# Early v products, DMA transposes for the second block, resident q and v weights, and parked q outputs in idle weight rows

## The chip, the cores and the metric

One core of one Trainium2 chip. The metric is the device time of one execution in microseconds (us); the time of a kernel is the median of its runs. A profiled span is about 2 us shorter than the time of the same run (730.3 of 732.26 for the kernel before).

The granted clock is TensorE's clock in the records, as a share of full speed: 1.0 is full.

Engines: PE is TensorE, DVE VectorE, ACT ScalarE, POOL GpSimd, SP SyncE (here it only issues DMAs).

## The reference

```python
xn = layernorm(x)                      # x: 1 x 2048 x 1024, bf16
q, k, v = split(xn @ wqkv)             # 32 heads of 32
logits = q . k[pos - 2*w], w = 0..7    # sliding window, 8 keys at distance 2
s = (softmax(logits * 32**-0.5) @ v[pos - 2*w]) @ wo
g = silu((silu(xn @ w1) * (xn @ w3)) @ w2)   # hidden width 3584
return x + s * g
```

## The kernel before

The rows of x are worked on in four blocks of 512 (numbered 0 to 3). Every large product is done with Strassen-Winograd: seven half-size products in place of eight, at the price of operand sums on DVE. PE computes q, k and v for blocks 0 and 1, then for blocks 2 and 3, then the MLP for the first 1024 rows, then the second. The attention is not on PE: its scores and weighted values are elementwise work on DVE, laid between other DVE instructions.

Outputs of blocks 1 to 3 are *parked* in DRAM, through a pool of staging buffers (`k4`) that everything else uses too:

```python
def park(t, c, j0, name):                       # t: 0 q, 1 k, 2 v;  c: block
    tl = k4(name, (2, CH), BF16)
    dst = (q_dram, k_dram, v_dram)[t][c, :, j0:j0 + 2, :]
    def fin():
        nc.sync.dma_start(out=dst, in_=tl[:])
    return tl[:], fin
```

How attention work gets its place in DVE's order is settled when the program is built. A generator yields the estimated time of each attention instruction; each PE group grants a budget, and other DVE work is charged to it as `owed`:

```python
def qkv_sums(w0, w1_, st):
    ...                                         # four sums on DVE
    pace["owed"] += 4.5
def bg(us):
    ...
    pace["credit"] += us - pace["owed"]
    pace["owed"] = 0
    with priority(BG), behind("v"):
        while pace["credit"] > 0:
            t = next(att_it)                    # places one DVE instruction
            ...
            pace["credit"] -= t
```

Of the kernel before, what the change touches and what calls it, by code (L numbers as in the profile page):

```python
# [8 lines left out]
FP32 = mybir.dt.float32  # L9
BF16 = mybir.dt.bfloat16  # L10
# [7 lines left out]
def kernel(  # L18
# [11 lines left out]
    nc = tc.nc  # L30
    P = 128
    S, D, F = 2048, 1024, 3584
    Dh, W, DIL = 32, 8, 2
    KT = D // P
    KH = KT // 2
    CH = 512
    NC = S // CH
    NST = CH // P
# [4 lines left out]
    NJ = 8  # L43
    NR = 4
    BG = 1000000
    I = range(2)
# [36 lines left out]
        out=ident[:], in_=ident[:], compare_op=ALU.not_equal, fill=1.0,  # L83
# [5 lines left out]
        out=ones4[:], in_=ones4[:], compare_op=ALU.is_ge, fill=0.0,  # L89
# [3 lines left out]
        out=ones4[:], in_=ones4[:], compare_op=ALU.is_ge, fill=0.0,  # L93
# [5 lines left out]
        out=maskb[0:32], in_=maskb[0:32], compare_op=ALU.is_ge, fill=-1.0e9,  # L99
# [9 lines left out]
    oT = keep.tile([P, 2, NJ, CH], BF16, name="oT")  # L109
    o16 = oT[:].bitcast(FP16)  # L110
    pb = keep.tile([P, W, P], BF16, name="pb")
    xT = keep.tile([P, 3, KH, CH], BF16, name="xT")
    xs = keep.tile([P, 4, KH, CH], FP16, name="xs")
# [4 lines left out]
    def slot(i, shape, dt=BF16, at=0):  # L118
        n = 1
        for x in shape:  # L120
            n *= x
        v = wring[:, i:i + max(1, n // SLOT), :].rearrange("p s n -> p (s n)")[:, at:at + n]
        v = v if dt is BF16 else v.bitcast(dt)
        d = "abc"[:len(shape)]
        return v.rearrange(f"p ({' '.join(d)}) -> p {' '.join(d)}", **dict(zip(d, shape)))

    def rows(f0, n, dt=BF16):
        v = h_sb[:, f0:f0 + n, :].rearrange("p f n -> p (f n)")
        return v if dt is BF16 else v.bitcast(dt)
# [4 lines left out]
    def k4(name, shape=(2, CH), dt=FP32):  # L134
        return kk.tile([P, *shape], dt, tag="k4", name=name)
# [93 lines left out]
    xt = {}  # L229
# [11 lines left out]
    def ln_dve(c, sts):  # L241
        xt4 = xt[c]
        n = len(sts)
        mv = small.tile([P, n, nc.vector.BN_AGGR_DIM], FP32, tag="mv")
        rstd = small.tile([P, n], FP32, tag="rstd")
        for i, st in enumerate(sts):
            stats = small.tile([P, 2, nc.vector.BN_STATS_DIM], FP32, tag="stats")
            for h in range(2):
                nc.vector.bn_stats(out=stats[:, h, :], in_=xt4[:, st, h * 512:(h + 1) * 512])
            nc.vector.bn_aggr(out=mv[:, i, :], in_=stats[:])  # L250
        nc.scalar.activation(out=rstd[:], in_=mv[:, :, 1], func=ACTF.Sqrt, bias=eps_t[:], scale=1.0)
        nc.vector.reciprocal(out=rstd[:], in_=rstd[:])
        for i, st in enumerate(sts):
            nc.vector.tensor_scalar(
                out=xt4[:, st, :], in0=xt4[:, st, :], scalar1=mv[:, i, 0:1], scalar2=rstd[:, i:i + 1],
                op0=ALU.subtract, op1=ALU.mult,
            )
# [18 lines left out]
    def ln_tp(c, st, dst, busy=0):  # L276
        tp = bank2(f"tp{c}_{st}")
        spin(tp, busy)
        for kt in range(KT):
            nc.tensor.matmul(  # L280
                tp[:, kt // KH, (kt % KH) * P:(kt % KH + 1) * P], lhsT=xt[c][:, st, kt * P:(kt + 1) * P], rhs=ident[:],
                start=(kt % KH == 0), stop=(kt % KH == KH - 1), skip_group_check=True,
            )
        cols = slice(st * P, (st + 1) * P)
        for d, s_ in dst:
            nc.scalar.copy(out=d[..., cols], in_=tp[:, s_].rearrange("p a (k t) -> p a k t", k=KH))
        return tp
# [5 lines left out]
    def xn_sums(b11, b21, b12, b22, o):  # L293
        nc.vector.tensor_sub(o[:, 0], b12, b11)
        nc.vector.tensor_sub(o[:, 1], b22, o[:, 0])
        nc.vector.tensor_sub(o[:, 2], b22, b12)
        nc.vector.tensor_sub(o[:, 3], b21, o[:, 1])
# [9 lines left out]



    def qkv_sums(w0, w1_, st):  # L310
        lo = lambda w: w.rearrange("p k (c two j) -> p k c two j", two=2, j=4)[:, :, :, 0]
        hi = lambda w: w.rearrange("p k (c two j) -> p k c two j", two=2, j=4)[:, :, :, 1]
        a11, a21, a12, a22 = lo(w0), hi(w0), lo(w1_), hi(w1_)
        s1, s2, s4 = [s.rearrange("p k (c j) -> p k c j", j=4) for s in st]
        s3 = hi(w0.bitcast(FP16))
        nc.vector.tensor_add(s1, a21, a22)
        nc.vector.tensor_sub(s2, s1, a11)
        nc.vector.tensor_sub(s4, a12, s2)
        nc.vector.tensor_sub(s3, a11, a21)
        pace["owed"] += 4.5  # L320

    def qkv_A(w0, w1_, st, g):
# [5 lines left out]
        sp = lambda q: [[sv[q][:, k, 2 * g + i, :] for k in range(KH)] for i in I]  # L328
        return pick(v0, 0), pick(v1, 0), pick(v1, 1), sp(0), sp(1), pick(v3, 1), sp(2)

    def park(t, c, j0, name):
        tl = k4(name, (2, CH), BF16)
        dst = (q_dram, k_dram, v_dram)[t][c, :, j0:j0 + 2, :]

        def fin():
            nc.sync.dma_start(out=dst, in_=tl[:])

        return tl[:], fin

    def qkv_dst(t, c, j0):  # L340
        if c == 0:
# [15 lines left out]
    def qkv_seven(t, b, w0, w1_, st, mid=None, snaps=None):  # L357
        c0, c1 = 2 * b, 2 * b + 1
        for g in range(2):
            cp = lambda c, j0: qkv_copy(t, c, j0)  # L360
            seven(f"q{t}{b}{g}", qkv_A(w0, w1_, st, g), Bq[b],
                  cp(c0, 2 * g), cp(c1, 2 * g), cp(c1, 4 + 2 * g), cp(c0, 4 + 2 * g),
                  None if snaps is None else snaps[g])
            if mid is not None:
                mid(g)

    def qkv_load(t, h, wt):
        anchor["wq"] = nc.sync.dma_start(out=wt, in_=wqkv_r[:, h * 4:(h + 1) * 4, t * D:(t + 1) * D])
        return wt
# [5 lines left out]
    def att_tile(shape, dt, name):  # L375
        return att.tile([P, *shape], dt, tag="a8", name=name)
# [6 lines left out]
    sc = {}  # L383
# [19 lines left out]
    def scores(c, ws):  # L403
        q = qt[c]
        if c not in sc:
            sc[c] = att_tile((W, CH), BF16, f"Es{c}"), att_tile((NJ, CH), BF16, f"pt{c}")
        E, p_t = sc[c]
        for w in ws:
            o = HALO - DIL * w
            nc.vector.tensor_mul(p_t[:], q[:], kT[:, :, o:o + CH])  # L410
            yield 2.3
            nc.vector.tensor_add(p_t[:, 0:4, :], p_t[:, 0:4, :], p_t[:, 4:8, :])  # L412
            yield 1.25
            nc.vector.tensor_add(p_t[:, 0:2, :], p_t[:, 0:2, :], p_t[:, 2:4, :])
            yield 0.7
            nc.vector.tensor_add(E[:, w, :], p_t[:, 0, :], p_t[:, 1, :])
            yield 0.45
# [102 lines left out]
    pace = {"n": 0, "credit": 0, "owed": 0}  # L520
# [36 lines left out]

    tiles = {}

    free = [0, 1, 2, 3, 4, 6, 7, 8, 9]  # L560
    half = [0, 1]
    held = {}

# [403 lines left out]
    wq0 = qkv_load(0, 0, slot(2, (4, D)))  # L967
    x_load(1)
    wq1 = qkv_load(0, 1, slot(6, (4, D)))
    for st in range(NST):  # L970
        (ln_act if st == 2 else ln_dve)(0, [st])
    qt[0] = att_tile((NJ, CH), BF16, "qt0")
    tps = [ln_tp(0, st, [], busy=(5, 0, 1, 1)[st]) for st in range(NST)]
    for a in I:
        for st in range(NST):
            (nc.vector.tensor_copy if st < 2 else nc.scalar.copy)(
                out=xT[:, a, :, st * P:(st + 1) * P], in_=tps[st][:, a].rearrange("p (k t) -> p k t", k=KH),
            )
    wk0 = qkv_load(1, 0, slot(8, (4, D)))
    wk1 = qkv_load(1, 1, rows(0, 4).rearrange("p (k n) -> p k n", k=4))  # L980
    sk = rows(4, 6, FP16).rearrange("p (q k n) -> p q k n", q=3, k=4)
    sk = [sk[:, q] for q in range(3)]
    b12 = k4("b12", (KH, CH), BF16)
    x_load(2)
    ln_dve(1, [0, 1])
    ln_dve(1, [2, 3])

    sq = rows(20, 6, FP16).rearrange("p (q k n) -> p q k n", q=3, k=4)
    sq = [sq[:, q] for q in range(3)]
# [1 line left out]
    Bq = B0, B_of(xT1[0], xT1[1], xT1[3], xs1)  # L991
    def tp1(*sts):
        for st in sts:
            ln_tp(1, st, [(b12[:].unsqueeze(1), slice(0, 1)), (xT[:, 2:3], slice(1, 2))])

    for t, (w0, w1_, ws) in enumerate(((wq0, wq1, sq), (wk0, wk1, sk))):
        first_two(f"f{t}", [qkv_A(w0, w1_, ws, g) for g in range(2)], B0[0], B0[1],
                  snap[2 * t:2 * t + 2], [qkv_copy(t, 0, 2 * g) for g in range(2)],
                  *((lambda: None, 4) if t == 0 else (lambda: tp1(2, 3), 0)))
        if t == 0:  # L1000
            tp1(0, 1)
    qkv_sums(wq0, wq1, sq)
    xn_sums(xT[:, 0], xT[:, 1], b12[:], xT[:, 2], xs)
    qkv_sums(wk0, wk1, sk)
    qkv_seven(0, 0, wq0, wq1, sq, None, snap[0:2])
    x_load(3)
# [4 lines left out]

    tr(2)

    wv = [slot(2 + 4 * h, (4, D)) for h in I]
    sva = slot(0, (2, 4, CH), FP16)
    sv = [sva[:, 0], sva[:, 1], rows(10, 2, FP16).rearrange("p (k n) -> p k n", k=4)]

    def before_v(g):
        if g == 0:
            for h in I:  # L1020
                qkv_load(2, h, wv[h])
            tr(3)
        else:
            with behind("v"):
                qkv_sums(*wv, sv)

# [5 lines left out]
                xn_sums(xT1[0], xT1[1], xT1[2], xT1[3], xs1)  # L1032
        w2_step()
    pace["n"] = PACE[0]
    qkv_seven(2, 0, *wv, sv, step0)
    pace["n"] = PACE[1]
    qkv_seven(1, 1, wk0, wk1, sk, step)
    flush()
    wq0 = qkv_load(0, 0, slot(8, (4, D)))
    wq1 = qkv_load(0, 1, rows(0, 4).rearrange("p (k n) -> p k n", k=4))  # L1040
    qkv_sums(wq0, wq1, sk)
    qkv_seven(2, 1, *wv, sv, step)
    qkv_seven(0, 1, wq0, wq1, sk, step)
    flush()
# [46 lines left out]
```

## Time and profile before

| | kernel before |
|---|---|
| time, median of 3 runs | 732.37 us (732.24 to 732.5) |
| span of the profiled run, granted clock | 730.3 us, 0.998 |
| PE busy | 714.2 us, 98% |
| DVE busy | 624.2 us, 85% |
| first qkv product / first product that needs the x sums | 13.25 / 29.57 us |
| first MLP product / first down-projection product | 161.46 / 417.75 us |
| last PE work ends | 724.30 us |

The times of the lower rows are starts of PE rows in order of time. The prediction shows the page, the waits and the rows that it rests on.

In a row in order of time the columns are start (us), duration (us), engine, line of the program, operation, output<-inputs, shapes and count; a bracket at the end gives the idle time just before and what ended it (`issue`: nothing that the row itself names). L149 is the helper that issues every product, L159 the helper for ACT copies, so tiles tell what a row is: `am`, `bm`, `em` are accumulators of the MLP's up products, `aq`, `bq`, `eq` (and `af`) of qkv, `da`, `db`, `de` of the down projection.

### The profile page before, as it was taken

To read this page: it belongs to the slowest core of one execution; us is meant where nothing else is said; L and a number is where in the kernel's file an instruction comes from. 1 tells how busy PE (TensorE), PEld (TensorE's weight loads), DVE (VectorE), ACT (ScalarE), POOL (GpSimd) and SP (SyncE) were. 2 spreads that over 40 slices of the span, in tenths; PEclk is the share of its full clock that TensorE was granted. 3 is DMA by queue.
4 is the path that set the end of the run, shared out by engine and by line. 5 is a ranking of instruction groups with operands and counts; after the bars stand their busy time and mean duration, and the time that the engine had idled before them with its cause. 6 is when DMAs were issued, how large, how long until landed. Compare 5 with 4: busy or idle time off the path is not lost.

```text
span 730.3 us, 8739 instructions
## 1 busy us (share of the span) xinstructions
PE 714.2 (98%) x3312; PEld 345.8 (47%) x3367; DVE 624.2 (85%) x677; ACT 314.5 (43%) x328; POOL 99.3 (14%) x159
## 2 busy tenths in 40 slices
PE   7999999999999999999999999999999999999996
PEld 4655665654444444444444444444444444444442
DVE  7994688878798879878989899969859999979984
ACT  5744343437554546654545411123454555120233
POOL 0000000010400110142202010010345000510011
PEclk9999999999999999999999999999999999999999
DMA  9379148877756452467755745549799453666505
GB/s 321 140 177 286 57 147 281 254 210 262 200 204 231 143 175 87 141 194 242 231 174 191 240 156 186 178 162 375 188 283 326 136 159 102 192 190 203 179 5 111
DMA packets 117610, 140.82 MB, mean 193 GB/s; under 512 B 14273, under 2 KB 91073, under 8 KB 116929
## 3 DMA queue, kind: packets, MB, share of 16 engines
q1 hardware_dynamic: 103984, 101.47, 44.9%
q0 software_dynamic: 13584, 38.81, 17.2%
q8 instruction: 26, 0.43, 0.3%
q14 instruction: 16, 0.12, 0.1%
HBM read 98.30 MB, written 38.80 MB: 188 GB/s over the span
## 4 chain that ended last, share of the span: by engine, by line
PE 71%; DVE 18%; DMA 4%; issue 3%; ACT 3%; SPq 1%; POOL 0%; DVEq 0%; ACTq 0%; POOLq 0%
PE bm L149 17%; PE am L149 11%; PE em L149 11%; PE db L149 7%; PE bq L149 5%; PE de L149 4%; DVE pt L410 4%; PE eq L149 4%; PE da L149 3%; PE aq L149 3%; PE wb L149 2%; DVE pt L412 2%; PE we L149 2%; PE wa L149 2%; DMA q_dram<-pk 1%
## 5 line engine op out<-in xcount | busy, mean ns | idle before, releaser
L149 PEld LDWEIGHTS <-wring 128*128 128x128 f16 (+1 forms) x1920 | 201.7, 105 | 216.4 <-issue 5.2
L149 PEld LDWEIGHTS <-h_sb 128*128 128x128 f16 (+1 forms) x1088 | 114.0, 105 | 121.7 <-issue 1.0
L149 PE MATMUL bm<-xs,wring 128*128 128x512 f16 x504 | 117.3, 379 | 0.5 <-DVE h_sb L661 0.3
L149 PE MATMUL am<-xT,wring 128*128 128x512 bf16 x322 | 78.8, 379 | 0.9
L410 DVE TENSOR_TENSOR pt<-qt,kT 128x4096 bf16<-128x4096 bf16 x32 | 73.2, 2288 | 0.7
L149 PE MATMUL db<-wring,h_sb 128*128 128x512 f16 x336 | 73.2, 379 | 0.0
L465 DVE TENSOR_TENSOR BC<-Ep,vT 128x2048 bf16<-128x2048 bf16 x56 | 67.0, 1218 | 0.2
L646 DVE TENSOR_TENSOR um<-em,um 128x1024 f32<-128x1024 f32 x28 | 34.2, 1222 | 19.9 <-PE em L149 12.9
L648 ACT ACTIVATE g<-um 128x1024 bf16<-128x1024 f32 x28 | 29.6, 1057 | 49.7 <-DVE um L646 49.7
L149 PE MATMUL da<-wring,h_sb 128*128 128x512 bf16 x219 | 48.9, 379 | 0.3
L451 POOL DMA_DIRECT2D Ep<-pb x64 | 37.9, 600 | 25.5 <-DVE pb L447 18.5
L149 PE MATMUL bm<-h_sb,wring 128*128 128x512 f16 x168 | 39.7, 379 | 0.0
L149 PE MATMUL em<-xs,wring 128*128 128x512 f16 x168 | 39.7, 379 | 0.0
L412 DVE TENSOR_TENSOR pt<-pt 128x2048 bf16<-128x2048 bf16 x32 | 39.1, 1221 | 0.5
L475 DVE TENSOR_TENSOR oT<-oT,BC 128x2048 bf16<-128x2048 bf16 x32 | 39.1, 1220 | 0.5
L149 PE MATMUL em<-xT,wring 128*128 128x512 bf16 x161 | 39.2, 379 | 0.3
L159 ACT COPY bm<-am 128x1024 f32<-128x1024 f32 x28 | 28.0, 999 | 26.1 <-PE am L149 26.1
L159 ACT COPY pm<-em 128x1024 f32<-128x1024 f32 x28 | 28.4, 1013 | 19.3 <-PE em L149 19.2
L159 ACT COPY um<-bm 128x1024 f32<-128x1024 f32 x28 | 28.4, 1013 | 18.6 <-PE bm L149 18.2
L667 ACT CAST g<-bm 128x1024 bf16<-128x1024 f32 x28 | 28.3, 1010 | 17.6 <-PE bm L149 17.6
L351 DVE TENSOR_TENSOR pk<-eq,uq 128x1024 bf16<-128x1024 f32 x12 | 14.7, 1222 | 23.7 <-PE eq L149 13.2
L661 DVE TENSOR_TENSOR h_sb<-bm,pm 128x1024 bf16<-128x1024 f32 x21 | 25.6, 1218 | 5.3 <-PE bm L149 5.3
(176 smaller groups left out, 965.3 us busy)
## 6 DMA issues: line engine op xcount, KB each, us to landing
wring<-in_B_w_dram SPq DMA_DIRECT2D x61, 512.0 KB, 4.4
wring<-t_dram SPq DMA_DIRECT2D x16, 512.0 KB, 5.1
t_dram<-wring POOLq DMA_DIRECT2D x14, 512.0 KB, 4.5
wring<-in_A_wqkv_dram SPq DMA_DIRECT2D x6, 1024.0 KB, 8.0
wring<-t_dram SPq DMA_DIRECT2D x16, 384.0 KB, 5.5
wring<-in_B_w_dram SPq DMA_DIRECT2D x12, 384.0 KB, 4.7
wring<-in_A_x_dram SPq DMA_DIRECT2D x16, 256.0 KB, 6.1
Ep<-pb POOLq DMA_DIRECT2D x64, 64.0 KB, 4.9
```

The source lines that it names most:

```text
L149: anchor["pe"] = nc.tensor.matmul(ps, lhsT=lhs[k], rhs=rhs[k], start=(first and k == 0), stop=(k == n - 1), skip_group_check=not first,)
L159: nc.scalar.copy(out=out_, in_=in_)
L351: anchor["v"] = nc.vector.tensor_add(d, ps[:], a[0][:])
L410: nc.vector.tensor_mul(p_t[:], q[:], kT[:, :, o:o + CH])
L412: nc.vector.tensor_add(p_t[:, 0:4, :], p_t[:, 0:4, :], p_t[:, 4:8, :])
L451: nc.gpsimd.dma_start(out=pr[c][r:P:NR, :, sq * P:(sq + 1) * P], in_=pb[sq * 32:(sq + 1) * 32, :, :])
L465: nc.vector.tensor_mul(dst, E[:, w, :].unsqueeze(1).to_broadcast([P, n, CH]), vT[:, js, o:o + CH])
L475: nc.vector.tensor_add(A, A, B if w0 else C)
L646: v = nc.vector.tensor_add(su2[:], pe[:], su2[:])
L648: nc.scalar.activation(out=hl["g"][:, :, CH:], in_=su2[:], func=ACTF.Silu)
L661: anchor["v"] = nc.vector.tensor_add(h[:, :, CH:], pb[:], sp5[:])
L667: nc.scalar.copy(out=hl["g"][:, :, 0:CH], in_=pb[:])
```

## The change

Its intent: give PE work at the start that does not need block 1's transposed x (the first v products), so that the transposes of that block can be taken off PE and done by DMA meanwhile; load v weights at the start and q weights only once (they were loaded twice); and stage parked q outputs of blocks 2 and 3 in weight rows of `h_sb` that nothing uses any longer, so that the common staging buffers have less to wait for. The core of the diff:

```diff
-    def qkv_sums(w0, w1_, st):
+    def qkv_sums(w0, w1_, st, again=False):
         ...
+        if again:                       # s3 is still there from the first time
+            nc.vector.tensor_sub(s2, a22, s3)
+            nc.vector.tensor_add(s1, s2, a11)
+            nc.vector.tensor_sub(s4, a12, s2)
+            pace["owed"] += 3.4
+            return
 ...
+    spare = [0, 1, 2, 3, 10, 11, 0, 1]
     def park(t, c, j0, name):
-        tl = k4(name, (2, CH), BF16)
+        tl = k4(name, (2, CH), BF16)[:] if t or c < 2 else rows(spare.pop(0), 1).rearrange("p (j n) -> p j n", j=2)
 ...
-            nc.sync.dma_start(out=dst, in_=tl[:])
+            (nc.gpsimd if c == 1 else nc.sync).dma_start(out=dst, in_=tl)
 ...
-    free = [0, 1, 2, 3, 4, 6, 7, 8, 9]
+    free = [8, 9, 0, 1, 4, 2, 3, 6, 7]
 ...
+    wve = [att_tile((4, D), BF16, f"wve{h}") for h in I]
+    vsn = att_tile((2, 2, CH), FP32, "vsn")
 ...
-    b12 = k4("b12", (KH, CH), BF16)
+    b12 = rows(12, 2).rearrange("p (k n) -> p k n", k=KH)
+    TPE = ()                            # x tiles still transposed on PE: none
+    qkv_load(2, 0, wve[0][:])
+    for st in range(NST):
+        ln_dve(1, [st])
+        if st not in TPE:
+            for a, d in ((0, b12), (1, xT[:, 2])):
+                nc.sync.dma_start(out=d[:, :, st * P:(st + 1) * P], in_=xt[1][:, st, a * CH:(a + 1) * CH], transpose=True)
+        if st == 1:
+            qkv_load(2, 1, wve[1][:])
     x_load(2)
-    ln_dve(1, [0, 1])
-    ln_dve(1, [2, 3])
 ...
-    for t, (w0, w1_, ws) in enumerate(((wq0, wq1, sq), (wk0, wk1, sk))):
+    snap += [vsn[:, 0], vsn[:, 1]]
+    for t, (w0, w1_, ws) in enumerate(((wq0, wq1, sq), (wk0, wk1, sk), (wve[0][:], wve[1][:], sk))):
 ...
-    qkv_seven(2, 0, *wv, sv, step0)
+    qkv_seven(2, 0, *wv, sv, step0, snap[4:6])
 ...
-    wq0 = qkv_load(0, 0, slot(8, (4, D)))
-    wq1 = qkv_load(0, 1, rows(0, 4).rearrange("p (k n) -> p k n", k=4))
-    qkv_sums(wq0, wq1, sk)
+    qkv_sums(wq0, wq1, sk, True)
```

Cut: the pool order (`free`) is shown, the reuse of `oT` for the first score temporaries and the places where v weights were loaded before are not.

More of the change, by code (lines that the diff above doesn't have):

```diff
@@ L329, in qkv_A @@
         return pick(v0, 0), pick(v1, 0), pick(v1, 1), sp(0), sp(1), pick(v3, 1), sp(2)
+    spare = [0, 1, 2, 3, 10, 11, 0, 1]
     def park(t, c, j0, name):
-        tl = k4(name, (2, CH), BF16)
+        tl = k4(name, (2, CH), BF16)[:] if t or c < 2 else rows(spare.pop(0), 1).rearrange("p (j n) -> p j n", j=2)
         dst = (q_dram, k_dram, v_dram)[t][c, :, j0:j0 + 2, :]
         def fin():
-            nc.sync.dma_start(out=dst, in_=tl[:])
-        return tl[:], fin
+            (nc.gpsimd if c == 1 else nc.sync).dma_start(out=dst, in_=tl)
+        return tl, fin
     def qkv_dst(t, c, j0):
@@ L405, in scores @@
         if c not in sc:
-            sc[c] = att_tile((W, CH), BF16, f"Es{c}"), att_tile((NJ, CH), BF16, f"pt{c}")
+            sc[c] = att_tile((W, CH), BF16, f"Es{c}"), oT[:, 0] if c == 0 else att_tile((NJ, CH), BF16, f"pt{c}")
         E, p_t = sc[c]
@@ L982 @@
     sk = [sk[:, q] for q in range(3)]
-    b12 = k4("b12", (KH, CH), BF16)
+    b12 = rows(12, 2).rearrange("p (k n) -> p k n", k=KH)
[5 more added lines that the diff above has]
+            for a, d in ((0, b12), (1, xT[:, 2])):
+                nc.sync.dma_start(
+                    out=d[:, :, st * P:(st + 1) * P], in_=xt[1][:, st, a * CH:(a + 1) * CH], transpose=True,
+                )
+        if st == 1:
+            qkv_load(2, 1, wve[1][:])
     x_load(2)
-    ln_dve(1, [0, 1])
-    ln_dve(1, [2, 3])
     sq = rows(20, 6, FP16).rearrange("p (q k n) -> p q k n", q=3, k=4)
@@ L993, in tp1 @@
         for st in sts:
-            ln_tp(1, st, [(b12[:].unsqueeze(1), slice(0, 1)), (xT[:, 2:3], slice(1, 2))])
-    for t, (w0, w1_, ws) in enumerate(((wq0, wq1, sq), (wk0, wk1, sk))):
+            ln_tp(1, st, [(b12.unsqueeze(1), slice(0, 1)), (xT[:, 2:3], slice(1, 2))])
+    snap += [vsn[:, 0], vsn[:, 1]]
+    for t, (w0, w1_, ws) in enumerate(((wq0, wq1, sq), (wk0, wk1, sk), (wve[0][:], wve[1][:], sk))):
         first_two(f"f{t}", [qkv_A(w0, w1_, ws, g) for g in range(2)], B0[0], B0[1],
                   snap[2 * t:2 * t + 2], [qkv_copy(t, 0, 2 * g) for g in range(2)],
-                  *((lambda: None, 4) if t == 0 else (lambda: tp1(2, 3), 0)))
-        if t == 0:
-            tp1(0, 1)
+                  *((lambda: None, 4) if t == 0 else (lambda: None, 0)))
+    tp1(*TPE)
     qkv_sums(wq0, wq1, sq)
-    xn_sums(xT[:, 0], xT[:, 1], b12[:], xT[:, 2], xs)
+    xn_sums(xT[:, 0], xT[:, 1], b12, xT[:, 2], xs)
     qkv_sums(wk0, wk1, sk)
@@ L1012 @@
     tr(2)
-    wv = [slot(2 + 4 * h, (4, D)) for h in I]
+    wv = [wve[h][:] for h in I]
     sva = slot(0, (2, 4, CH), FP16)
@@ L1019, in before_v @@
         if g == 0:
-            for h in I:
-                qkv_load(2, h, wv[h])
             tr(3)
-        else:
             with behind("v"):
```

## The prediction

The sum is 1.3 + 0.7 + 0.2 + 0.7 = 2.9 us, and 732.4 less that is 729.5 (taken as 729.6). From the trace of the kernel before: a pitch of 0.216 us for a product of 512 columns and of 0.056 us for a transpose on PE (0.89 us for 16), DMA transposes that landed 3.0 us (least) to 3.5 us (median) after issue, and 13.6 us to landing for the second k weight half.

> **What bounds the kernel now.** I read the page's busy shares and slices first, then the list of what TensorE waited for, then the time-ordered rows of PE, DVE and the SP queue up to 90 us, then the same rows from 140 to 182 us, because the diff touches only the q/k/v stage and the buffers handed on to the stage after it.
>
> From the page, busy share and slices:
> ```profile
> PE 714.2 (98%) x3312; PEld 345.8 (47%) x3367; DVE 624.2 (85%) x677; ACT 314.5 (43%) x328; POOL 99.3 (14%) x159
> PE   7999999999999999999999999999999999999996
> DVE  7994688878798879878989899969859999979984
> PEclk9999999999999999999999999999999999999999
> ```
> TensorE is busy everywhere except the first and last slice, at full granted clock. So only three things shorten the run: fewer PE instructions, a shorter start, or removal of PE bubbles. The waits of PE over the whole span show how much the last two can be:
> ```profile
> PE tp L280 <- DVE wring L254: 2.3, 1, 2.3
> PE warm L141 <- DVE warm L138: 1.3, 1, 1.3
> PE am L149 <- ACT bm L159: 0.7, 1, 0.7
> PE eq L149 <- DVE xs L294: 0.5, 1, 0.5
> PE bq L149 <- DVE pk L351: 0.3, 1, 0.3
> ```
> (columns: total us, times, longest.) The first two lie before 13 us, in the norm of the first block, which the change leaves alone. What remains is under 3 us of named waits in 717 us. That already limits the gain to well under 1%.
>
> PE in order of time, the q/k/v start and the k-to-v border:
> ```profile
> 13.25 7.07 PE L149 MATMUL af<-xT,wring 128*128 128x512 bf16 x32
> 20.15 1.06 PE L280 MATMUL tp<-ident,wring 128*128 128x128 bf16 x16
> 21.04 3.62 PE L149 MATMUL af<-xT,wring 128*128 128x512 bf16 x15
> 24.50 1.06 PE L280 MATMUL tp<-ident,wring 128*128 128x128 bf16 x16
> 29.57 2.35 PE L149 MATMUL eq<-xs,h_sb 128*128 128x512 f16 x10 [0.54 <-DVE xs L294]
> 65.21 1.02 PE L149 MATMUL bq<-xs,h_sb 128*128 128x512 f16 x4 [0.34 <-DVE pk L351]
> 66.35 1.92 PE L149 MATMUL eq<-xs,wring 128*128 128x512 f16 x8
> ```
> Start to start, 32 products of 512 columns take 20.15 - 13.25 = 6.90 us, 0.216 us each (a count of 15 or 7 is a lost record). The 16 transposes of a half block delay the next group by 21.04 - 20.15 = 0.89 us and 25.40 - 24.50 = 0.90 us.
>
> SP queue and DVE, why the k-to-v border stalls, and the later wait for a parked output:
> ```profile
> 54.52 3.32 SPq L291 DMA_TRANSPOSE h_sb<-wring  x1
> 58.75 5.74 SPq L291 DMA_TRANSPOSE h_sb<-wring  x3
> 62.13 1.23 DVE L351 TENSOR_TENSOR pk<-eq,uq 128x1024 bf16<-128x1024 f32 x1 [6.35 <-DMA k_dram<-pk]
> 148.98 1.23 DVE L351 TENSOR_TENSOR pk<-eq,uq 128x1024 bf16<-128x1024 f32 x1 [4.10 <-DMA q_dram<-pk]
> 177.74 1.45 PE L149 MATMUL bm<-xs,wring 128*128 128x512 f16 x6 [0.30 <-DVE h_sb L661]
> ```
> Parked outputs queue on SP behind transposes, their staging buffer comes free late, and DVE idles 6.35 us; PE feels about 0.8 us of it around 65 us. The 4.10 us of DVE idle at 149 us costs PE nothing at once.
>
> [...]
>
> **The change part by part.**
>
> 1. Transposes of block 1 off PE. It removes 32 matmuls of 128 columns: 0.89 + 0.90 = 1.8 us of PE, on the path. It also takes eight 0.6 us casts off ACT (4.9 us, not on the path).
>
> 2. First v products early. The instruction order holds 32 v products right after k's. They are not extra work: v's own stage loses the same 32. But q's first product that needs the operand sums (eq) moves 6.90 us later. Before, it stood at 29.57 after a wait of 0.54 us (0.71 us against the normal pitch). The new no-stall time is 13.25 + 3 x 6.90 = 33.95 us; the like-for-like time of before is 29.57 + 6.90 = 36.47 us. So parts 1 and 2 give at most 2.5 us. What could spoil it:
>  - Accumulators: there are four; v's first product reuses that of q's first, which ACT empties only after four snapshots and one k copy. With ACT copies of 1.01 us following PE from 15 us, this one ends at about 27.4 us against PE's 27.05: an estimated stall of 0.4 us.
>  - Transposed x: the eight DMA transposes (half size) stand on SP behind seven megabytes of x and weights, and the second v half stands between them. At the 385 GB/s that the DMA slices of before show up to 21 us, the seven megabytes end at 22 to 24 us; at the 210 to 290 GB/s seen during transposes each half of them takes about 2 us and the v weights between them 2.7; the last land at about 31 to 32.5 us. DVE then makes the first sum (1.2 us) by 32.5 to 33.7. PE asks at about 34.4. It fits, with about 1 us to spare.
>  - DVE after that: it would have finished all weight sums at 29.4 us (its order from 12.6 us: eight stats at 0.62, four scalings at 0.55, eight weight sums at 1.14), so it idles 2 to 3 us, then does three more sums and seven stats of block 2 before q's first park. That park ends an estimated 9.4 us after eq starts, where the PE tail asks at 8.6: stall 0.4 to 0.9 us, and as much again a group later. Before had 0.3 us there.
>  Net of parts 1 and 2: 2.5 - 0.4 - (0.3 to 1.5) = 0.6 to 1.8 us, middle 1.3.
>
> 3. v weights resident, parks of block 1 on POOL. At the k-to-v border the v sums now stand before the last two k parks in DVE's order, weights are long there, and SP holds only transposes. The 0.5 + 0.28 us of PE bubbles at 65 us should go: 0.7 us.
>
> 4. q weights kept. It removes two 1 MB loads (112 to 121 us) and one of four sums (1.21 us of DVE at 128 us). PE had a 0.28 us hole at 117 us near them: 0.2 us.
>
> 5. q outputs of blocks 2 and 3 parked in idle weight rows. DVE's 4.10 us wait at 149 us and ACT's waits of 2 us nearby go. PE waited then for nothing, but DVE arrives earlier at the next stage, where PE lost 0.3 + 0.46 + 0.8 us from 165 to 180 us: I credit half, 0.7 us.
>
> 6. Attention's first scores now wait for the snapshot buffer, and the second query block for a v weight buffer. DVE's order places the scores right after v's parks, as before. No PE cost expected.
>
> Sum: 1.3 + 0.7 + 0.2 + 0.7 = 2.9 us, so 732.4 - 2.9 = 729.5. I take 729.6.
>
> **The rivals.** (a) The DMA queue becomes the bound at the start: the transposes land 3 us or more later than my estimate because the second v half delays the last four, and everything behind waits. For it: DMA is saturated from 10 to 20 us (share 1.05), SP is in order and transposes there have blocked it for 3.3 us. Against: PE is given 6.9 us more of work that needs none of it. It would eat the whole gain: 732 to 734. (b) Everything hides perfectly: DMA in time, no DVE stalls, all bubbles at 65 and 165 to 180 us gone: 2.5 + 0.3 + 0.8 + 0.3 + 1.5 = 5.4 us, 727.0. (c) DVE merely shifts its deficit: the time saved early returns as a wait of PE on DVE near 420 to 490 us, where the chain of waits runs through score products. DVE is busy 85% but PE waited only 0.5 us there, so it costs nothing before and little after: 731 to 732. (d) POOL parks land slower and hold the staging buffers: k's parks on SP took 5.7 us, a group lasts 8.6 us; harmless unless POOL needs over 8 us.
>
> **Range and chances.** 727.6 to 732.2 holds rival (b) nearly and the mild forms of (a) and (c). Over 2% faster would need 14.6 us, about three times all bubbles plus the removed instructions: chance 0.005. Over 2% slower needs a new stall of 14.6 us: 0.01. Within 2%: 0.985.
>
> **What would show it.** PE rows: no transposes after 13 us; 96 products unbroken from 13.25 to about 34.4 us with a hole under 0.5 us at 27; eq at 34 to 35 us, its wait (if any) on the sums behind a DMA transpose (rival a if over 1.5 us). At the k-to-v border no PE hole. No DVE wait on q parks near 145 us. If eq starts later than 36.5 us, parts 1 and 2 are worth nothing and I am wrong on them; if PE rows from 90 to 730 us have new holes of more than 1 us, I am wrong on parts 4 to 6.

## More of the kernel before

When a block's weighted values have read `vT`, the last 64 columns are copied to its front (the halo), and the next block's v is loaded behind them:

```python
def halo(t, js):
    nc.gpsimd.tensor_copy(out=t[:, js, 0:HALO], in_=t[:, js, CH:CH + HALO])
def fetch_v(c, js):
    ...
    halo(vT, js)
    anchor["pool"] = nc.gpsimd.dma_start(out=vT[:, js, HALO:], in_=v_dram[c, :, js])
```

The MLP keeps its hidden activations in `h_sb` (28 rows). Until it starts, the same rows hold qkv weights, sums and transposed x. Its first group writes rows 0 and 1:

```python
h = ... h_sb[:, f2, :]                          # f2 = rows 2*fb, 2*fb + 1
def e11(pa, ...):
    ...
    nc.scalar.activation(out=h[:, :, 0:CH], in_=pa[:], func=ACTF.Silu)
```

## The result, and the profile after

| | before | after |
|---|---|---|
| time, median | 732.54 us (732.24 to 732.9, 6 runs) | 736.96 us (734.98 to 738.03, 6 runs) |
| ratio after / before | | 1.0056, 95% from 1.0039 to 1.0073 |

A ratio here, and below, is the mean time of one kernel's fast runs over that of the other's in the same rounds, so it is not quite the ratio of the medians. The change is slower by 4 us where 3 us of gain were predicted, and its runs scatter over 3 us where those of before stay within 0.7.

From the page of the changed kernel, the busy shares and two rows of slices:

```profile
PE 715.9 (97%) x3281; PEld 345.0 (47%) x3335; DVE 622.9 (85%) x678; ACT 313.6 (43%) x324; POOL 111.9 (15%) x171
PE   8999999998999999999999999999999999999896
PEclk9999999999999999999999999999999999999899
```

PE has 31 recorded instructions fewer than before but is busy 1.7 us longer, and the slices show an 8 in the tenth place (166 to 184 us) and one in the third from the end (681 to 699 us); in the latter the granted clock falls too (0.74 from 684 to 696 us, below). PE runs slower there as well as idling. The waits of PE over the span (total us, times, longest) name both places:

```profile
PE de L149 <- ACT dsp L159: 3.6, 1, 3.6
PE bm L149 <- ACT um L159: 2.7, 1, 2.7
PE tp L280 <- DVE wring L254: 1.6, 1, 1.6
PE warm L141 <- DVE warm L138: 1.3, 1, 1.3
PE bq L149 <- DVE pk L359: 1.1, 2, 0.6
```

The first two are single waits that the kernel before does not have. Milestones (us) show when the time goes:

| PE milestone | before | after | after - before |
|---|---|---|---|
| first qkv product | 13.25 | 12.50 | -0.75 |
| first product with x sums, less 6.90 for the moved v products | 29.57 | 26.63 | -2.94 |
| first MLP product | 161.46 | 158.45 | -3.01 |
| first down-projection product | 417.75 | 417.77 | +0.02 |
| the late `de` products start | 663.62 | 662.75 | -0.87 |
| second half's wo product starts | 699.88 | 705.58 | +5.70 |
| last PE work ends | 724.30 | 730.00 | +5.70 |

So the start won 3 us in this trace (0.75 of it in when the first product happened to start), these 3 were lost between the MLP's first product and the down projection, and 6.6 (5.70 + 0.87) after 663 us.

**The start.** Rows of PE, of the SP queue and of DVE, changed kernel:

```profile
12.50 10.30 PE L149 MATMUL af<-xT,wring 128*128 128x512 bf16 x47
26.31 7.38 PE L149 MATMUL af<-xT,wve 128*128 128x512 bf16 x32
28.62 1.27 SPq L1000 DMA_TRANSPOSE xT<-wring  x1
31.50 1.23 DVE L294 TENSOR_TENSOR xs<-h_sb,xT 128x2048 f16<-128x2048 bf16 x1 [3.25 <-issue]
33.53 1.89 PE L149 MATMUL eq<-xs,h_sb 128*128 128x512 f16 x8
42.88 1.89 PE L149 MATMUL bq<-xs,wring 128*128 128x512 f16 x8 [0.55 <-DVE pk L359]
```

The last DMA transpose is issued at 28.62 us, DVE makes the first x sum at 31.50 (the view of these transposes names this sum as what waited for them, 3.2 us), and PE takes it at 33.53 without a wait: until then it was busy with the early v products. The eight transposes (four 128x128 tiles each) held the SP queue for 1.21 to 2.79 us each, from 15.52 us on. The price is the short wait at 42.88.

**The first hole, at 169 us.** Rows of the SP queue, ACT and PE, changed kernel:

```profile
162.93 0.32 SPq L344 DMA_DIRECT2D q_dram<-h_sb  x1
168.64 1.28 ACT L650 ACT_TABLE_LOAD   x1 [3.79 <-DMA q_dram<-h_sb]
169.94 1.02 ACT L650 ACTIVATE h_sb<-am 128x1024 bf16<-128x1024 f32 x1
170.86 1.01 ACT L159 COPY um<-bm 128x1024 f32<-128x1024 f32 x1
171.91 3.36 PE L149 MATMUL bm<-xs,wring 128*128 128x512 f16 x8 [2.70 <-ACT um L159]
```

The silu of the MLP's first group (L650) waits 3.79 us for a DMA that *reads* `h_sb`. The list of spare rows ends `..., 0, 1`: the last two parked q outputs lie in rows 0 and 1, and rows 0 and 1 are what this silu writes. The store of the last one is issued at 162.93 and ACT is free of it at 168.64, 5.7 us later; the DMA engines are 94% busy in these 6 us (the stretches below). In ACT's rows the copy `um` comes right behind this silu, at 170.86, and PE waits 2.70 us for it. The eight products after it then take 3.36 us instead of 1.89: another 1.47. In the kernel before nothing stood between:

```profile
168.64 1.89 PE L149 MATMUL bm<-xs,wring 128*128 128x512 f16 x8
169.16 1.02 ACT L642 ACTIVATE h_sb<-am 128x1024 bf16<-128x1024 f32 x1
```

**The second hole, at 681 us.** POOL, DVE and PE, changed kernel:

```profile
649.32 4.57 POOL L395 COPY vT<-vT 128x64 bf16<-128x64 bf16 x1 [30.44 <-DVE BC L473]
652.58 1.22 DVE L483 TENSOR_TENSOR oT<-oT,BC 128x2048 bf16<-128x2048 bf16 x1
654.19 0.77 POOL L409 DMA_DIRECT2D vT<-v_dram  x1 [0.30 <-POOL vT L395]
662.37 1.23 DVE L473 TENSOR_TENSOR oT<-Ep,vT 128x2048 bf16<-128x2048 bf16 x1 [8.58 <-DMA vT<-v_dram]
681.41 1.22 DVE L822 TENSOR_TENSOR dsp<-db,dsp 128x1024 f32<-128x1024 f32 x1
683.62 0.99 ACT L159 COPY dsp<-de 128x1024 f32<-128x1024 f32 x1
```

and the same place before:

```profile
649.13 1.17 POOL L387 COPY vT<-vT 128x64 bf16<-128x64 bf16 x1 [16.27 <-DVE BC L465]
650.60 0.77 POOL L401 DMA_DIRECT2D vT<-v_dram  x1 [0.30 <-POOL vT L387]
658.30 1.23 DVE L465 TENSOR_TENSOR oT<-Ep,vT 128x2048 bf16<-128x2048 bf16 x1 [4.65 <-DMA vT<-v_dram]
678.35 1.22 DVE L814 TENSOR_TENSOR dsp<-db,dsp 128x1024 f32<-128x1024 f32 x1
```

The same small halo copy, started at the same moment, takes 4.57 us instead of 1.17, and ends 0.09 us after the DVE instruction of 652.58 ends. Its v load is issued 3.6 us later, DVE resumes at 662.37 instead of 658.30, its backlog of values stands before the sum `dsp`, and PE waits 3.62 us for the ACT copy that comes after it.

Busy time of the engines by stretches (stretch, length, busy of PE, PEld, DVE, ACT, POOL, granted clock, DMA share, GB/s), changed kernel:

```profile
163.00:169.00 6.00, 5.93 (x28) 2.62 (x27) 6.00 (x10) 2.19 (x3) 0.53 (x1) 1.00 0.94 281
170.00:175.00 5.00, 3.09 (x8) 1.15 (x8) 1.60 (x2) 4.95 (x5) 0.00 (x0) 0.66 1.07 380
684.00:696.00 12.00, 11.28 (x39) 4.56 (x40) 11.29 (x10) 2.73 (x3) 0.00 (x0) 0.74 0.27 80
```

and before:

```profile
170.00:175.00 5.00, 4.95 (x24) 2.29 (x24) 5.00 (x8) 2.48 (x3) 0.00 (x0) 1.00 1.05 413
684.00:696.00 12.00, 11.95 (x57) 5.40 (x57) 11.97 (x11) 2.61 (x3) 0.00 (x0) 1.00 0.40 131
```

The first row is the time of the store, with DMA nearly full. In the 12 us after the second hole PE looks busy (11.28), but starts 39 products instead of 57, at a clock of 0.74. That busy time hides a loss of 3.0 us. The first hole shows the same: 8 products in 3.36 instead of 1.89 us, at a clock of 0.66 from 170 to 175 us. From 175 to 180 us and from 696 to 710 us the clock is 1.0 again. What makes it fall behind a hole the rows do not show, and e1 and e9 below have holes of 3.80 and 3.12 us without it.

### The profile page after: what moved, and what is told of

Same layout as the page of the kernel before. It is cut to its first block, busy times and chain, and to the rows that moved or that the text cites. A ratio compares the mean times of both kernels' runs of the same rounds, so it can differ in the third digit from the quotient of the medians.

```text
span 735.8 us, 8677 instructions
## 1 busy us (share of the span) xinstructions
PE 715.9 (97%) x3281; PEld 345.0 (47%) x3335; DVE 622.9 (85%) x678; ACT 313.6 (43%) x324; POOL 111.9 (15%) x171
## 4 chain that ended last, share of the span: by engine, by line
PE 75%; DVE 11%; issue 6%; DMA 4%; ACT 2%; POOL 2%; DVEq 0%; SPq 0%; ACTq 0%; POOLq 0%
PE bm L149 18%; PE am L149 12%; PE em L149 12%; PE bq L149 7%; PE db L149 7%; PE de L149 5%; PE eq L149 4%; PE da L149 3%; PE wb L149 2%; PE aq L149 2%; DVE stats L249 2%; PE we L149 2%; DVE BC L473 2%; PE wa L149 1%; DMA vT<-v_dram 1%
## 5 line engine op out<-in xcount | busy, mean ns | idle before, releaser
L149 PEld LDWEIGHTS <-wring 128*128 128x128 f16 (+1 forms) x1824 | 188.4, 103 | 211.8 <-issue 7.8
L149 PEld LDWEIGHTS <-h_sb 128*128 128x128 f16 (+1 forms) x1056 | 110.3, 104 | 124.8 <-issue 9.3
L149 PE MATMUL bm<-xs,wring 128*128 128x512 f16 x504 | 118.9, 383 | 2.9 <-ACT um L159 2.7
L418 DVE TENSOR_TENSOR pt<-qt,kT 128x4096 bf16<-128x4096 bf16 x24 | 54.9, 2290 | 0.7
L149 PE MATMUL de<-wring,h_sb 128*128 128x512 bf16 x108 | 27.4, 410 | 3.8 <-ACT dsp L159 3.6
L958 POOL DMA_DIRECT2D out_dram<-h_sb x12 | 15.1, 1511 | 100.3 <-DVE h_sb L957 100.2
```

What stands on the lines that cost most here:

```text
L149: anchor["pe"] = nc.tensor.matmul(ps, lhsT=lhs[k], rhs=rhs[k], start=(first and k == 0), stop=(k == n - 1), skip_group_check=not first,)
L418: nc.vector.tensor_mul(p_t[:], q[:], kT[:, :, o:o + CH])
L958: nc.gpsimd.dma_start(out=rows_, in_=g, accum_op=ALU.add)
```

## The experiments

The theory: two accidents, independent of each other. (1) Rows 0 and 1 in the list of spare rows give the first silu a write-after-read wait (a write that has to wait until an earlier read of the same place is done). (2) `pace["owed"] += 3.4`, where the four sums of before charged 4.5, moves attention work in DVE's order; with the new order the late halo copy on POOL runs beside other DVE instructions than before and takes 4.57 us instead of 1.17. Each hole then costs half to nearly as much again through the clock (1.47 us on 2.70, 3.0 on 3.62). Rivals: DVE merely pays back later what was gained early, so that removing one hole lets another one open; the clock falls by itself and the holes are incidental; one of the other parts (parks on POOL, DMA transposes, resident weights) is to blame.

Times below are median (range, runs); ratios are against the kernel before in the same rounds. All twelve gave correct results.

| run | time, us | ratio to before, 95% |
|---|---|---|
| e0_after_again, changed kernel again | 737.41 (734.72 to 738.98, 6) | 1.0053 (1.0034 to 1.0071) |
| e1_rows23 | 732.22 (730.71 to 734.41, 6) | 0.9983 (0.9965 to 1.0001) |
| e2_halo_dve | 731.78 (729.77 to 732.76, 6) | 0.9972 (0.9957 to 0.9987) |
| e3_both | 726.92 (726.88 to 728.75, 5) | 0.9916 (0.9901 to 0.9931) |
| e7_owed | 728.46 (727.23 to 729.38, 6) | 0.9930 (0.9914 to 0.9947) |
| e9_before_owed | 739.81 (737.48 to 740.46, 6) | 1.0080 (1.0063 to 1.0098) |
| e5_tpe | 734.98 (734.19 to 735.25, 5) | 1.0020 (1.0006 to 1.0034) |
| e8_q_k4 | 729.31 (728.82 to 732.75, 6) | 0.9953 (0.9934 to 0.9971) |
| e10_late_v | 735.64 (734.83 to 735.86, 6) | 1.0024 (1.0008 to 1.0041) |
| e6_sp | 727.38 (726.64 to 727.96, 5) | 0.9915 (0.9899 to 0.9931) |
| e12_halo_act | 728.22 (727.35 to 728.94, 6) | 0.9926 (0.9910 to 0.9941) |
| e11_again, same as e3_both | 727.93 (726.62 to 728.67, 6) | 0.9920 (0.9904 to 0.9935) |

The kernel before had medians of 733.5 (first four rows), 733.34 (next four) and 733.36 (last four).

**The changed kernel again.** No edit.

> The changed kernel as it is, to see whether its two holes in PE recur. Theory: the hole near 169 us (ACT's first silu waits for the store of the last parked q output, 2.7 us of PE idle and then 1.5 us lost to a lower clock) is a fixed wait and is there again, 2.5 to 3 us. The hole near 681 us (PE waits 3.6 us for ACT and DVE, then 3.0 us lost to a lower clock) hangs on a small copy on POOL that took 4.6 us where its fellows take 1.2; if that is chance, it is shorter or absent here and the time is about 733.5 to 735; if it follows from the order of the instructions it is there again. Rival (a slow chip or state): no holes, time spread over all matmuls. Time 735 to 738.

737.41 us. The halo copy took 4.57 us again, and PE waited 3.1 us at the second hole and 2.9 at the first. Both holes belong to the program; they are no accident of one execution.

**First hole alone.** The last two parks go to rows 2 and 3, which the MLP's first silu does not write.

```diff
-    spare = [0, 1, 2, 3, 10, 11, 0, 1]
+    spare = [0, 1, 2, 3, 10, 11, 2, 3]
```

> One edit to the changed kernel: the last two parked q outputs go to weight rows 2 and 3 instead of 0 and 1. Theory: the MLP's first output goes to rows 0 and 1 and had to wait for the store of the parked output out of them; with rows 2 and 3 the wait of ACT on that store goes, PE's 2.7 us hole at 169 us and the 1.5 us of lower clock behind it go, and by 190 us PE is 2.5 to 4 us ahead of the changed kernel. Time 2.5 to 4.5 us below the changed kernel if the late hole stays as it is. Rival (the hole belongs to DVE, which is late there anyway): the hole stays within 0.5 us under another name, time unchanged.

732.22 us, 5.2 less than the changed kernel on the same chip. The longest wait of PE:

```profile
PE de L149 <- ACT dsp L159: 3.8, 1, 3.8
```

The wait for `um` is gone, the late one stays. In this trace the late hole is longer (3.80 us) than in the changed kernel's, but no slow products follow it: the 27 rows behind it take 6.20 us, 27 before it took 6.21, and the granted clock of the span is 0.998, as in the kernel before. Whether a hole of this size costs clock differs from run to run.

**Second hole alone.** The v halo is copied by DVE itself and no longer by POOL.

```diff
     def fetch_v(c, js):
         ...
-        halo(vT, js)
+        nc.vector.tensor_copy(out=vT[:, js, 0:HALO], in_=vT[:, js, CH:CH + HALO])
```

> One edit to the changed kernel: the copies of the v halo columns (128x64, six of them) on DVE instead of POOL. Theory: the late hole comes from the POOL copy, which waited for DVE for 4.6 us at 649 us and made the v load and all DVE work behind it late; with the copy on DVE the load starts about 4 us earlier, DVE's wait for it falls from 8.6 to about 5 us, PE's wait of 3.6 us at 681 us and the 3 us of lower clock behind it go: 4 to 6.5 us below the changed kernel. Rival (the order of DVE's late work, moved by the change, is to blame): DVE gets the same work later anyway, PE's hole stays above 2 us.

731.78 us, 5.6 less. Two of PE's waits:

```profile
PE bm L149 <- ACT um L159: 2.9, 1, 2.9
PE de L149 <- ACT dsp L159: 1.2, 1, 1.2
```

The first hole stays, the late one shrinks to 1.2 us; the granted clock of the span is 0.996, against 0.992 in both traces of the changed kernel.

**Both repairs.** The two edits together ("the repaired kernel").

> Both edits of the two runs before. Theory: the two holes are independent and together more than the whole loss; without them the gain that was predicted appears: PE about 3 us ahead of the kernel before from 190 us on, and a time of 727.5 to 730.5. Rival (the gain is eaten by something else later, as DVE is loaded to 85%): a new hole of 2 us or more appears behind 190 us and the time is 731 to 734.

726.92 us: 10.5 less than the changed kernel. The two single effects, 5.2 and 5.6, add up to 10.8. So they are independent, and the rival of a deficit that returns elsewhere falls: with both repaired, nothing opened in their place. The span of the profiled run has granted clock 1.0; the longest waits of PE:

```profile
PE bq L149 <- DVE pk L359: 1.4, 2, 0.8
PE warm L141 <- DVE warm L138: 1.3, 1, 1.3
PE tp L280 <- DVE wring L254: 1.1, 2, 0.9
PE af L149 <- DMA wve<-in_A_wqkv_dram: 0.8, 1, 0.8
```

The rival of a clock that falls by itself falls too: without the two holes the clock of the span is 1.0. And at the place of the first hole ACT and PE are in step again:

```profile
168.22 1.02 ACT L650 ACTIVATE h_sb<-am 128x1024 bf16<-128x1024 f32 x1
171.15 1.89 PE L149 MATMUL bm<-xs,wring 128*128 128x512 f16 x8
```

**The budget, other way round.** Rows 2 and 3, the halo back on POOL, but the charge of before, 4.5, in the short branch. If the order of DVE's attention work is what harms, this alone must cure it.

```diff
             nc.vector.tensor_sub(s4, a12, s2)
-            pace["owed"] += 3.4
+            pace["owed"] += 4.5
```

> The changed kernel with the last two parked q outputs in rows 2 and 3 (as in the run of that name) and one more number: the second q sums book 4.5 us of DVE time against attention, as in the kernel before, instead of 3.4. That number places attention among DVE's other work when the program is ordered, and with 4.5 the order of DVE from the middle of the program on is again that of the kernel before, instruction for instruction. The halo copy stays on POOL. Theory (the 1.1 us moved the attention work, so that the late halo copy on POOL meets an unbroken run of DVE work): the late copy takes about 1.2 us, PE's late hole is under 0.5 us, time 726.5 to 728.5 as with the copy on DVE. Rival (the copy is slow for another reason that the change brought, such as the DMA traffic or POOL's new parks): it takes 4.6 us again and PE waits over 3 us, time 731 to 733.

728.46 us, and the late halo copy on POOL is short:

```profile
646.25 1.17 POOL L395 COPY vT<-vT 128x64 bf16<-128x64 bf16 x1 [17.71 <-DVE BC L473]
654.92 1.23 DVE L473 TENSOR_TENSOR oT<-Ep,vT 128x2048 bf16<-128x2048 bf16 x1 [4.15 <-DMA vT<-v_dram]
```

A number in a compile-time budget, which no engine ever sees, decides whether the second hole is there. (The time is 0.5 to 1.5 us above the repaired kernel's, whose ratios are 0.9916 and 0.9920 against 0.9930: no difference that the intervals tell.) A 0.5 us wait of PE for a sum (`dsu`) that the changed kernel had lost came back with the old order, so 3.4 has a small use there.

**The budget in the kernel before.** One line added to it, after its second q sums, so that they charge 3.4 there too. Nothing else of the change is in it.

```diff
     qkv_sums(wq0, wq1, sk)
+    pace["owed"] -= 1.1
```

> The kernel before with nothing but that number changed: its second q sums book 3.4 us instead of 4.5. No instruction is added or removed; the order of DVE from the middle on becomes that of the changed kernel. Theory: the late halo copy on POOL takes 4.6 us here too, PE waits 3 to 4 us for it near 680 us and runs 2 to 3 us at a lower clock after that: 4.5 to 6.5 us slower than the kernel before. Rival (the order alone does nothing): within 1 us of the kernel before.

739.81 us. The second hole appears in the old kernel:

```profile
654.85 4.57 POOL L387 COPY vT<-vT 128x64 bf16<-128x64 bf16 x1 [30.22 <-DVE BC L465]
689.68 6.20 PE L149 MATMUL de<-wring,h_sb 128*128 128x512 bf16 x28 [3.12 <-ACT dsp L159]
```

So it is caused by the budget and not by resident weights, DMA transposes or early v. The run also showed something that had not been expected, a hole of 4.92 us at 167 us:

```profile
166.28 1.23 DVE L351 TENSOR_TENSOR pk<-bq,pq 128x1024 bf16<-128x1024 f32 x1 [6.08 <-DMA q_dram<-pk]
167.56 3.57 PE L149 MATMUL bq<-h_sb 128*128 128x512 f16 x8 [4.92 <-DVE pk L351]
```

With this order the old staging of parked q outputs hurts: DVE waits 6.08 us for a buffer. The changed kernel has no such wait there; but e8 below has the same staging and the same charge, and though DVE waits 5.62 us for such a buffer at 160 us there, PE feels 1.41 of it and the run loses only about 2 us, so this hole belongs to the combination with the old kernel, and I have not taken it apart. Part of the 739.81 is this hole; only the late one says something of the changed kernel.

**Transposes back on PE.** Repaired kernel, with the 32 transposes of block 1 on PE after the 96 first products.

```diff
-    TPE = ()
+    TPE = (0, 1, 2, 3)
```

> The repaired kernel (rows 2 and 3, halo copy on DVE) with the transposes of block 1 back on PE, after the 96 first products. Theory: 32 transposes cost 1.8 us of PE, and ACT's eight casts behind them (0.6 us each, five on the path before the sums) make DVE's sums and q's first eq later by another 1 to 3 us: 728.7 to 731. Rival (DMA transposes cost what they save): within 0.7 us of the repaired kernel, 726.5 to 727.5.

734.98 us, some 4 us beyond what was expected. PE does its transposes in 1.95 us, but what follows it was not counted: ACT must cast them out, DVE stands meanwhile at statistics of x that has not landed (3.06 us), and PE waits.

```profile
33.05 1.95 PE L280 MATMUL tp<-ident,wring 128*128 128x128 bf16 x32
39.80 3.60 PE L149 MATMUL eq<-xs,h_sb 128*128 128x512 f16 x8 [4.80 <-DVE xs L294]
```

3.60 us for eight products, instead of 1.89, shows the clock loss once more (granted clock of the span 0.994, against 1.0 in the repaired kernel). This is one order of several (the kernel before had its transposes between the products, and waited only 0.5), so it does not price the DMA transposes; it shows that in this place they are needed.

**v's first products back in v's stage.** Repaired kernel, DMA transposes kept, 32 fewer products at the start.

```diff
-    vsn = att_tile((2, 2, CH), FP32, "vsn")
-    snap += [vsn[:, 0], vsn[:, 1]]
-    for t, (w0, w1_, ws) in enumerate(((wq0, wq1, sq), (wk0, wk1, sk), (wve[0][:], wve[1][:], sk))):
+    for t, (w0, w1_, ws) in enumerate(((wq0, wq1, sq), (wk0, wk1, sk))):
 ...
-    qkv_seven(2, 0, *wv, sv, step0, snap[4:6])
+    qkv_seven(2, 0, *wv, sv, step0)
```

> The repaired kernel (rows 2 and 3, halo copy on DVE) with v's first products back in v's own stage, all else kept: DMA transposes, resident v weights. Theory: the early v products are what hides the DMA transposes. Without them PE has work until about 27 us only, the transposes land at about 31 us and the sum behind them is ready at 32.7, so PE waits about 5 us for the sums near 28 to 33 us, and loses 1 to 3 us more to a lower clock: 731 to 735, of the gain of the repaired kernel nothing is left. Rival (the order of the products is indifferent, the gain is the transposes): within 1.5 us of the repaired kernel.

735.64 us. PE asks for the x sums 6 us too early:

```profile
33.52 3.60 PE L149 MATMUL eq<-xs,h_sb 128*128 128x512 f16 x8 [6.22 <-DVE xs L294]
```

The first product with x sums starts at 33.52, in the changed kernel at 33.53, but not for the same reason: here PE waits for the sum that DVE starts at 32.24, there DVE started it at 31.50 and PE was still busy with the early v products. These fill what is otherwise a wait, and behind that wait eight products take 3.60 us (granted clock 0.56 from 30 to 36 us). With e5, no order that was tried shows one of the two parts paying without the other.

**q parks back in the common staging.** DVE halo, all parks through `k4`.

```diff
-        tl = k4(name, (2, CH), BF16)[:] if t or c < 2 else rows(spare.pop(0), 1)...
+        tl = k4(name, (2, CH), BF16)[:]
```

> The changed kernel with the halo copy on DVE and all parked outputs in the common staging buffers again, none in weight rows. Theory: no wait for rows 0 and 1, so PE's hole at 169 us goes; DVE and ACT wait 2 to 4 us for staging buffers near 145 us as in the kernel before, and some PE holes of 0.3 to 0.8 us near 165 to 180 us are back: 727 to 729, so that the staging in weight rows is worth at most 1 us against the repaired kernel and cost 4 to 5 us as written. Rival (the staging is what made the gain): 730 or more.

729.31 us, some 2 us above the repaired kernel (726.92 and 727.93). PE's waits for parks are 2.4 us in three, instead of 1.4 and 1.1 in two:

```profile
PE bq L149 <- DVE pk L359: 2.4, 3, 1.4
```

Staging in weight rows is worth about 2 us when the rows are chosen well. As it was, with rows 0 and 1, it gave that up and more: e2, which differs from this run in the staging alone, took 731.78 us (0.9972 against 0.9953, a loss of 1.4 to 2.5 us that the intervals do not quite tell from none). The 5 us of e1 are the distance between the two choices of rows. The two repaired runs were made on another occasion than this one; the ratios (0.9953 against 0.9916 and 0.9920) say the same of the 2 us.

**Parks from SP instead of POOL.** Repaired kernel.

```diff
-            (nc.gpsimd if c == 1 else nc.sync).dma_start(out=dst, in_=tl)
+            nc.sync.dma_start(out=dst, in_=tl)
```

> The repaired kernel with the twelve parked outputs of block 1 stored from SP again, in no other order of PE or DVE. Theory: they queue behind SP's transposes of blocks 2 and 3 (14 us of SP time from 43 to 58 us), the staging buffers come free late, DVE waits several us for them and PE 0.5 to 1.5 us between 45 and 70 us: 727.5 to 729. Rival (the issuer is indifferent[...]): within 0.4 us of the repaired kernel.

727.38 us, ratio 0.9915 against 0.9920 of the repaired kernel in the same rounds: no difference. In this kernel the issuer of these parks does not matter, and a gain from it was wrongly supposed.

**Halo on ACT.** Repaired kernel, the v halo as a copy on ACT.

```diff
-        nc.vector.tensor_copy(out=vT[:, js, 0:HALO], in_=vT[:, js, CH:CH + HALO])
+        nc.scalar.copy(out=vT[:, js, 0:HALO], in_=vT[:, js, CH:CH + HALO])
```

> The changed kernel with rows 2 and 3 and the v halo copies on ACT, in place of POOL. Theory (POOL's copy is what is held up while DVE runs without a break[...]): the late copy takes under 0.4 us, the load behind it is issued about 4 us earlier than in the changed kernel, no late hole: within 1 us of the repaired kernel, 726.5 to 728. Rival (it only helped that DVE's order got a step in it): a copy of over 3 us and a hole of 3 us again, 731 to 733.

728.22 us, against 727.93 with the halo on DVE in the same rounds: no difference that the intervals (0.9926 and 0.9920, each with 0.0016 on either side) tell. The late copy is short:

```profile
646.59 0.24 ACT L408 COPY vT<-vT 128x64 bf16<-128x64 bf16 x1 [3.45 <-DVE BC L473]
```

This cure is therefore that the copy leaves POOL, not that DVE does it.

**The repaired kernel once more.** No edit to e3_both.

> The repaired kernel a second time, to see that its time holds: 726.5 to 729, at least 4 us below the kernel before of the same rounds.

727.93 us, ratio 0.9920 against 0.9916 before: it beats both kernels, on two occasions, by 5.4 us and more. Among its remaining early losses is PE's wait for the first v weights, 0.8 us in one trace and 1.5 in the other.

**What stays open.** Why the copy on POOL ends at some ends of DVE instructions and not at others. In the six v halo copies of each of six traces that were looked at, a copy that ran beside DVE ended about 0.09 us after the end of some DVE instruction. Mostly it was the one that ran when the copy began (1.17 or 1.29 us), in some cases the one after it (2.14 us in e7), and at the second hole the fourth (4.57 us in all four traces with that order), after which DVE had nothing left to run. What distinguishes these ends is not visible in the rows.

## Why the prediction was wrong

**Parts 1 and 2, transposes off PE and early v: right.** No transposes stand on PE behind the first block, and the x sums came as worked out (31.50, at the early end of the estimate) so that PE did not wait. From the first product to the first with sums it took 21.03 us; less the 6.90 of v that is 14.13 against 16.32 before, a gain of 2.2, where the terms up to there made 2.1 (2.5 less 0.4 at the accumulators; the 32 v products took 7.22 us instead of 6.90, so 0.3 was lost there). The stall at q's first park was 0.71 us, within 0.4 to 0.9; the second one, "as much again a group later", did not come. (The net of these parts is misadded: 0.4 to 0.9 and as much again, less 0.3, is 0.5 to 1.5 and not 0.3 to 1.5, so 0.6 to 1.6 remain, middle 1.1.) Rival (a), late DMA, did not happen in this trace, and e10 shows that it would without the early v. But a mild form that the prediction had not costed did happen in six of the other traces with this start (e1, e3, e7, e8, e11, e12): PE waited 0.25 to 1.50 us for the v weights.

**Parts 3 and 4: the bubbles went, others came.** The holes of about 0.8 us at the k-to-v border are gone, but the new one at 42.9 us (0.71) and one of 0.73 us at 110 us (PE on a park; DVE had waited 0.24 us for a k store just before) took as much. From the first product with sums to the MLP it took 131.89 us before, 124.99 less the moved v products, and 124.92 after: nothing gained. The prediction had 0.9 here, and counted the stall at 42.9 against parts 1 and 2.

At the MLP's start PE was 3.0 us ahead. The prediction's whole sum was 2.9, of which 0.7 was to come later. So far the total fits, with the start giving more and parts 3 and 4 less. That it fits so closely is partly luck: of the ten traces with this start this one is the furthest ahead. The others reach the MLP's first product at 158.76 to 160.59 us, 0.9 to 2.7 us ahead of the one trace of the kernel before, and e9, with the start of that kernel, reaches it at 160.97.

**Part 5: the failed step.** "I credit half, 0.7 us" took the rows to be idle. DVE's wait of 4.10 us for a staging buffer near 145 us did go (it now waits there 1.14 and 0.43 us, both for PE), though a like one of 3.94 us, for the store of a v output, now stands at 132 us; PE waits for neither. But the question to ask of a staging buffer, who writes there next and how soon, was not asked of the last two entries of the list. They are read by a store 5.7 us long and written by the next stage's first silu. In place of +0.7 the runs show a loss of 4.2 us in the trace (2.70 of wait and 1.47 of clock; 5.2 in the medians). With rows 2 and 3 the stretch from the first MLP product to the first of the down projection takes 255.03 us in the repaired kernel, against 256.29 before: a gain of 1.3, more than was credited (in e8, with the common staging, it takes 256.59).

**Part 6: the other failed step.** "DVE's order places the scores right after v's parks, as before. No PE cost expected." Part 4 had seen the removed sum as 1.21 us of DVE and not as a change of the budget by 1.1, which shifts all later attention work by some instructions. Late in the program the new order makes a copy of 1.17 us take 4.57, and that cost 6.6 us in the profiled run (3.62 of wait and 3.0 of clock), 5.6 in the medians. Rival (c), a wait on DVE later, is near to this in kind, but its reason (a DVE deficit) is refuted by e3: DVE has no less work (623.3 us busy in e3, 622.9 in the changed kernel), and the hole is gone.

**What no part of the sum had: the clock.** Both holes were followed by slow products, which added 1.47 us to 2.70 and 3.0 us to 3.62. In other traces holes of this size added nothing: behind 3.80 us in e1 27 products, and behind 3.12 us in e9 (late) 28, took 6.20 us. That may add to the scatter of the changed kernel's six runs (734.98 to 738.03 us), but this is not shown: in the later rounds the kernel before, without such holes, scatters as widely (731.88 to 735.49). A range that considers holes has to consider this second cost.

The prediction's own test for it was right: "if PE rows from 90 to 730 us have new holes of more than 1 us, I am wrong on parts 4 to 6". Holes of 2.70 and 3.62 us stand there. And rival (b), everything hides, 727.0 us, is in number what the repaired kernel reaches (726.92 and 727.93), but not in kind: PE still waits 1.4 and 1.1 us for parks there. Nor do the traces show where all of that gain lies: between the traced runs of the two kernels (732.26 and 728.75 us, the latter the slowest of its five) PE's last work ends only 3.1 us earlier: 0.95 us by the MLP's start, 1.26 more up to the down projection, 0.89 after it.

## What to carry to other kernels

Before a region is called free, look for its next writer as well as its last reader: here a store that read it held up that writer for 5.7 us from its issue, at a DMA share of 0.94. Where a compile-time budget sets the order of background work, a change of a weight in it is a change of the whole later order, and has to be compared instruction by instruction up to the end. On a PE that is busy 98%, look at the granted clock behind each hole: busy time hid slow products here (8 in 3.36 us instead of 1.89 at a clock of 0.66), and two small holes and what followed them turned a gain of 5 to 7 us into a loss of 4.
